# DMA transposes, another spread of the attention units, and a last tile in two halves, in a fused attention and feed-forward kernel

## The chip, the cores and the metric

The kernel runs on one core of one Trainium2 chip. A time is the device time of one execution in microseconds (us). Each run is fast or slow; slow means over 1.5% above the fastest run of the same kernel. Ratios below are taken between fast runs alone; the medians and ranges printed beside them are of all runs, and where slow runs matter they are called that. A profile is of one execution, and its span is a little shorter than the device time: for the kernel before, the profiled execution spans 176.4 us.

## The reference

The input x has 2048 rows of 448 columns. Attention and feed-forward both read the same normalised x, and their results are multiplied.

```python
def _layernorm(x, axis=-1, eps=1e-5):
    m = jnp.mean(x, axis=axis, keepdims=True)
    v = jnp.var(x, axis=axis, keepdims=True)
    return (x - m) / jnp.sqrt(v + eps)
# ... (setup: x is (1, 2048, 448) bf16; wqkv (448, 1344); wo (448, 448); w1 (448, 1792); w2 (1792, 448)) ...
def reference(A_x, A_wqkv, A_wo, B_x, B_w1, B_b1, B_w2, B_b2):
    def _A_ref(x, wqkv, wo):
        B, S, D = x.shape
        H = 16; Dh = D // H
        W, dil = 8, 2
        qkv = (lambda x, *d: x.transpose(*d))((x @ wqkv).reshape(B, S, 3, H, Dh), 2, 0, 3, 1, 4)
        # ... each position attends to 8 positions, two apart, itself and backwards; softmax; times v ...
        return (lambda x, *d: x.transpose(*d))(o, 0, 2, 1, 3).reshape(B, S, D) @ wo
    def _B_ref(x, w1, b1, w2, b2):
        h = jnp.einsum("bsd,df->bsf", x, w1) + b1
        h = _gelu(h)
        return jnp.einsum("bsf,fd->bsd", h, w2) + b2
    x = A_x
    xn = _layernorm(x, axis=-1)
    s = _A_ref(xn, A_wqkv, A_wo)
    g = _silu(_B_ref(xn, B_w1, B_b1, B_w2, B_b2))
    return x + s * g
```

## The kernel before

TensorE (PE) multiplies, ScalarE (ACT) does exponentials, GELU and some copies, VectorE (DVE) the remaining elementwise work, and SyncE (SP) issues the DMAs. The first three, and GpSimd (POOL) with its few constants, follow a hand-written order; SyncE does not, so that the scheduler may move its DMAs. Rows are handled in 16 tiles of 128, in four chunks of four tiles. Even and odd rows are stored apart, so that the dilated attention becomes one over neighbours. It is cut into 17 "units" of 121 queries.

TensorE needs the normalised x with columns on the partitions, so every tile is transposed into `xnT`. For chunk 0 this happens in the prologue. For chunks 1 to 3, the kernel before does it with TensorE, inside the feed-forward block of the chunk before, and VectorE copies the result out of PSUM, the memory that TensorE's products are written to.

All loads but two tiles of x are issued by SyncE, and the trace has them in the order of the program. The sixteen small loads of the output weights `wo` are last among them:

```python
    for dst, c0, c1 in ((wv, 2 * D, 3 * D), (wraw, 0, 2 * D)):
        nc.sync.dma_start(dst[:, 0:3, 0:c1 - c0], A_wqkv[0:384, c0:c1].rearrange("(k p) f -> p k f", p=P))
        nc.sync.dma_start(dst[:64, 3, 0:c1 - c0], A_wqkv[384:448, c0:c1])
    nc.sync.dma_start(b1t[:], B_b1.rearrange("(m f) -> f m", f=P))
    for c0, c1 in ((0, F // 2), (F // 2, F)):
        nc.sync.dma_start(w1[:, 0:3, c0:c1], B_w1[0:384, c0:c1].rearrange("(k p) f -> p k f", p=P))
        for r in (0, 64):
            nc.sync.dma_start(w1[r:r + 64, 3, c0:c1], B_w1[384:448, c0:c1])
        if c0 == 0:
            nc.sync.dma_start(x_sb[1][:, :, :], dram_rows(x_par, 4, 4))
    nc.sync.dma_start(w2[:, :, :], B_w2.rearrange("(m p) c -> p m c", p=P))
    nc.sync.dma_start(b2bc[:], B_b2.rearrange("(o d) -> o d", o=1).to_broadcast((P, D)))
    nc.sync.dma_start(x_sb[2][:, :, :], dram_rows(x_par, 8, 4))
    nc.sync.dma_start(x_sb[3][:, :, :], dram_rows(x_par, 12, 4))
    # ... constants ...
    for g in range(4):
        for h in range(4):
            r = (4 * g + h) * DH
            nc.sync.dma_start(wo[32 * h + 1:32 * h + 1 + DH, g, :], A_wo[r:r + DH, :])
```

The normalisation, the transpose and its copy, and the first reader of the transposed chunk:

```python
    def ln_apply(t):
        nc.vector.tensor_scalar(xnb[t % 4][:, 0:D], xt(t), mv[:, t, 0:1], rstd[:, t:t + 1],
                                op0=ALU.subtract, op1=ALU.mult)

        nc.vector.tensor_copy(xnb[t % 4][:, D:512], xnb[t % 4][:, D - 64:D])

    def ln_tr(t):
        pT = psB.tile([P, KT, P], BF16, name="pT", tag="B")
        for kt in range(KT):
            nc.tensor.transpose(pT[:, kt, :], xnb[t % 4][:, kt * P:(kt + 1) * P], ident[:])
        return pT

    def ln_put(t, pT, copy):
        copy(xnT[:, :, LEAD + t * P:LEAD + (t + 1) * P], pT[:, :, :])
    # ...
    def qk_job(c, g, which, copy):
        ps = psB.tile([P, CH], F32, name="ps_qk", tag="B")
        for kt in range(KT):
            nc.tensor.matmul(ps[:, :], wqk[:, kt, 16 * which + 4 * g:16 * which + 4 * g + 4, :],
                             xnT[:, kt, LEAD + c * CH:LEAD + (c + 1) * CH],
                             start=(kt == 0), stop=(kt == KT - 1))
        copy((qT, kT)[which][:, g, LEAD + c * CH:LEAD + (c + 1) * CH], ps[:, :])
```

One feed-forward block. `gelu` runs on ScalarE, and the products for the next pair of columns can only begin when a PSUM buffer of an earlier pair has been read. `wos` is a list of output tiles that TensorE takes in between:

```python
    def feed_forward_1(c, ps, wos):

        nc.scalar.preload_act_table_set(SET_GELU)
        nx = 4 * (c + 1)
        gelu(0, ps)
        for k in range(0, MT // 2, 2):
            if k:
                ps = ffn1_even(c, k)
                gelu(k, ps)
            if k + 1 < MT // 2:
                ps = ffn1_odd(c, k + 1)
                gelu(k + 1, ps)
            if c + 2 < NC and k < 4:
                ln_stats(nx + 4 + k)
                ln_stats(nx + 5 + k)
            if k in (2, 4):
                if c + 1 < NC:
                    for j in (k - 2, k - 1):
                        ln_put(nx + j, ln_tr(nx + j), nc.vector.tensor_copy)
                if c:
                    silu_job(4 * (c - 1) + k - 2)
                    silu_job(4 * (c - 1) + k - 1)
            for _ in range(2):
                if k >= (2 if c == 3 else 4) and wos:
                    wo_job(wos.pop(0))
        nc.scalar.preload_act_table_set(SET_EXP)
        if c + 2 < NC:
            ln_rstd(nx + 4, 4)
```

An output tile and the second half of an attention unit. `stream_shuffle` copies the softmax sums out of PSUM, ScalarE inverts them with Ln and Exp, and VectorE multiplies:

```python
    def wo_job(t):
        wo_put(t, wo_mm(t))
    # ...
    def qk_unit(b, between=lambda: None):
        # ... 16 score products into two PSUM pairs S, exponentials and masks into E ...
    def av_unit(b, E):
        psO = psB.tile([P, 4, P], F32, name="psO", tag="B")
        for g in range(4):
            for h in range(4):
                nc.tensor.matmul(psO[32 * h:32 * h + 32, g, 0:QW], vw[:, b, 4 * g + h, :],
                                 E[:, h, g, 0:QW], start=True, stop=True)
        n = min(QB, S - QB * b)
        den = work.tile([P, 4, QB], F32, name="den", tag="den", bufs=2)
        nc.vector.stream_shuffle(den[:, :, 0:n], psO[:, :, 0:n], [0] * 32)

        def norm():
            nc.scalar.activation(den[:, :, 0:n], den[:, :, 0:n], ACT.Ln)
            nc.scalar.activation(den[:, :, 0:n], den[:, :, 0:n], ACT.Exp, scale=-1.0)
            nc.vector.tensor_tensor(out=oT[:, :, QB * b:QB * b + n], in0=psO[:, :, 0:n],
                                    in1=den[:, :, 0:n], op=ALU.mult)
        return norm
```

The main loop: a feed-forward block, then the attention units, with the second feed-forward product (`ffn2_job`), the last q and k products and the v products beside them. Three phases take five units each, and two are left for the tail:

```python
        ps = ffn1_even(0, 0)
        for t in range(4, 8):
            ln_apply(t)

        units = iter(range(NB))
        for c in range(3):
            feed_forward_1(c, ps, [[], [0, 1], [2, 3, 4, 5]][c])
            n = c + 1
            beside = [lambda: q_job(n, 3), lambda: k_job(n, 3), lambda: v_job(4 * n), lambda: v_job(4 * n + 1)]
            if c == 2:
                beside[1] = lambda: (k_job(3, 3), v_job(12))
                beside[2] = lambda: v_job(13)
                beside[3] = lambda: v_job(14)
            for g in range(3):
                q_job(n, g)
                k_job(n, g, nc.vector.tensor_copy)
            norm = lambda: None
            for i in range(4):
                b = next(units)
                E = qk_unit(b)
                norm()
                ffn2_job(4 * c + i)
                beside[i]()
                if n + 1 < NC:
                    ln_apply(4 * n + 4 + i)
                norm = av_unit(b, E)
            b = next(units)
            va, vb = 4 * n + 2 + (c == 2), 4 * n + 3 + (c == 2)
            E = qk_unit(b, lambda: v_job(va))
            v_job(vb)
            norm()
            ps = ffn1_even(n, 0)
            norm = av_unit(b, E)
            norm()
        feed_forward_1(3, ps, [6, 7, 8, 9, 10])
        ffn2_job(12)
        E = qk_unit(15)
        g12 = silu_exp_job(12)
        ffn2_job(13)
        g12()
        s11 = wo_mm(11)
        norm = av_unit(15, E)
        wo_put(11, s11)
        E = qk_unit(16)
        g13 = silu_exp_job(13)
        norm()
        y14 = ffn2_job(14, False)
        s12 = wo_mm(12)
        norm = av_unit(16, E)
        g13()
        ffn2_put(14, y14)
        wo_put(12, s12)
        s13 = wo_mm(13)
        norm()
        nc.scalar.preload_act_table_set(SET_GELU)
        wo_put(13, s13)
        silu_job(14)
        y15 = ffn2_job(15, False)
        s14 = wo_mm(14)
        s15 = wo_mm(15)
        ffn2_put(15, y15)
        wo_put(14, s14)
        silu_job(15)
        wo_put(15, s15)
```

The softmax here doesn't subtract the row's maximum and nothing guards it: scores larger than these inputs give would overflow.

## Time and profile before

| kernel before | value |
|---|---|
| device time, median of 3 runs | 177.59 us (177.31 to 180.35, the last a slow run) |
| span of the profile | 176.4 us |
| TensorE busy | 163.9 us, 93% |
| ScalarE, VectorE busy | 71%, 68% |
| start of the q products of chunk 1 | 31.00 us |
| start of the GELU of the last feed-forward block | 143.01 us |
| first scores of the tail, last VectorE instruction | 155.63 us, 173.55 us |

The last three rows are read from the chain of waits and from the timeline of ScalarE.

The page of the profile also cuts the span into 40 slices. Each digit is the busy share of TensorE in tenths, and in the second row the granted clock of TensorE in tenths of full speed. From the kernel before:

```profile
PE   7698999999999989999999989999999999999480
PEclk9999999999999999999999999999999999999998
```

A reader should see that after the first four slices (17.6 us) TensorE is hardly ever free before the tail, and that its recorded clock stays at nine tenths or more until the last slice. This record doesn't show the slow start: the first eight products of 512 columns take 3.48 us, 0.43 us each instead of the 0.22 of later ones, while the view by windows gives a clock of 1.00 from 0.80 to 4.80 us.

### The profile page before, as it was taken

To read this page: it belongs to the slowest core of one execution; us is meant where nothing else is said; L and a number is where in the kernel's file an instruction comes from. 1 tells how busy PE (TensorE), PEld (TensorE's weight loads), DVE (VectorE), ACT (ScalarE), POOL (GpSimd) and SP (SyncE) were. 2 spreads that over 40 slices of the span, in tenths; PEclk is the share of its full clock that TensorE was granted. 3 is DMA by queue.
4 is the path that set the end of the run, shared out by engine and by line. 5 is a ranking of instruction groups with operands and counts; after the bars stand their busy time and mean duration, and the time that the engine had idled before them with its cause. 6 is when DMAs were issued, how large, how long until landed. Compare 5 with 4: busy or idle time off the path is not lost.

```text
span 176.4 us, 3278 instructions
## 1 busy us (share of the span) xinstructions
PE 163.9 (93%) x1324; PEld 75.6 (43%) x1324; DVE 120.0 (68%) x269; ACT 124.7 (71%) x196; POOL 4.5 (3%) x16
## 2 busy tenths in 40 slices
PE   7698999999999989999999989999999999999480
PEld 2343344444454334445454335444555434445140
DVE  6854846667886655977886415987677413978693
ACT  3853397646889699646879699534788699978650
POOL 6030000000000000000000000000000000000000
PEclk9999999999999999999999999999999999999998
DMA  5999972000000000100000000210000000120011
GB/s 145 232 239 320 362 245 50 3 0 4 0 4 0 0 0 4 52 0 4 0 0 6 0 0 0 73 34 0 4 0 0 4 2 0 52 78 30 0 52 52
DMA packets 10991, 9.03 MB, mean 51 GB/s; under 512 B 2593, under 2 KB 10977, under 8 KB 10977
## 3 DMA queue, kind: packets, MB, share of 16 engines
q1 hardware_dynamic: 10688, 8.61, 16.6%
q10 hardware_dynamic: 288, 0.23, 0.4%
q8 instruction: 10, 0.16, 0.4%
q14 instruction: 5, 0.03, 0.1%
HBM read 7.00 MB, written 1.84 MB: 50 GB/s over the span
## 4 chain that ended last, share of the span: by engine, by line
PE 68%; ACT 15%; DVE 7%; SPq 4%; DMA 3%; issue 2%; DVEq 0%
PE ps_y L257 23%; PE ps_h L224 13%; PE ps_qk L188 13%; PE ps_s L288 6%; ACT E L317 4%; PE S L312 3%; PE ps_v L203 3%; DMA x<-in_A_x_dram 3%; PE ps_h L233 3%; ACT hT L239 3%; ACT den L336 2%; PE psO L328 2%; SPq L106 2%; ACT den L335 2%; DVE den L332 2%
## 5 line engine op out<-in xcount | busy, mean ns | idle before, releaser
L317 ACT ACTIVATE E<-S 128x976 bf16<-128x976 f32 x34 | 32.0, 985 | 19.6 <-PE S L312 18.7
L257 PE MATMUL ps_y<-w,hT 128*128 128x448 bf16 x224 | 45.1, 353 | 0.7 <-DVE y L264 0.7
L224 PE MATMUL ps_h<-xnT,w 128*128 128x512 bf16 x168 | 40.3, 380 | 1.5 <-ACT hT L239 1.5
L239 ACT ACTIVATE hT<-ps_h,b1f 128x512 bf16<-128x512 f32 x56 | 33.9, 708 | 2.6 <-PE ps_h L233 2.2
L188 PE MATMUL ps_qk<-xnT,wqk 128*128 128x512 bf16 x128 | 29.4, 379 | 0.6 <-DVE qT L191 0.6
L257 PEld LDWEIGHTS <-hT 128*128 128x128 bf16 x224 | 20.8, 98 | 20.2 <-issue 0.9
L319 DVE TENSOR_TENSOR E<-E,mk_gen 128x976 bf16<-128x976 bf16 x30 | 19.9, 666 | 7.6 <-ACT E L317 7.6
L224 PEld LDWEIGHTS <-w 128*128 128x128 bf16 x168 | 15.4, 98 | 21.4 <-issue 5.7
L337 DVE TENSOR_TENSOR oT<-psO,den 128x484 bf16<-128x484 f32 (+1 forms) x17 | 11.2, 661 | 12.7 <-ACT den L336 12.7
L188 PEld LDWEIGHTS <-wqk 128*128 128x128 bf16 x128 | 12.4, 98 | 15.5 <-issue 1.4
L269 DVE SCALAR_TENSOR_TENSOR g<-th,y 128x448 bf16<-128x448 bf16 x14 | 8.2, 621 | 14.1 <-ACT th L268 14.1
L203 PE MATMUL ps_v<-wv,xnT 128*128 128x448 bf16 x68 | 15.2, 353 | 0.1
L288 PE MATMUL ps_s<-wo,oT 128*128 128x448 bf16 x64 | 13.8, 353 | 1.6 <-DVE oT L337 1.6
L335 ACT ACTIVATE den<-den 128x484 f32<-128x484 f32 (+1 forms) x17 | 10.4, 610 | 5.4 <-DVE den L332 5.4
L191 DVE CAST qT<-ps_qk 128x512 bf16<-128x512 f32 x16 | 10.9, 682 | 3.5 <-PE ps_qk L188 3.5
L156 DVE BATCH_NORM_STATS2 st<-x 128x6 f32<-128x448 bf16 x16 | 9.8, 610 | 5.0 <-DMA x<-in_A_x_dram 5.0
L208 ACT CAST vw<-ps_v 128x448 bf16<-128x448 f32 x17 | 9.1, 536 | 3.9 <-PE ps_v L203 3.8
L332 DVE STREAM_SHUFFLE den<-psO 128x484 f32<-128x484 f32 (+1 forms) x17 | 11.8, 696 | 0.0
L233 PE MATMUL ps_h<-xnT,w 64*128 64x512 bf16 x56 | 10.5, 384 | 0.4
L336 ACT ACTIVATE den<-den 128x484 f32<-128x484 f32 (+1 forms) x17 | 10.3, 605 | 0.5
L264 DVE TENSOR_TENSOR y<-ps_y,b2bc 128x448 f32<-128x448 f32 x16 | 9.9, 618 | 0.9 <-PE ps_y L257 0.8
L294 DVE SCALAR_TENSOR_TENSOR sg<-ps_s,g 128x448 bf16<-128x448 f32 x16 | 9.9, 618 | 0.2
(60 smaller groups left out, 126.5 us busy)
## 6 DMA issues: line engine op xcount, KB each, us to landing
out_dram<-o_t SPq DMA_DIRECT2D x16, 112.0 KB
w<-in_B_w_dram SPq DMA_DIRECT2D x1, 1568.0 KB
w<-in_B_w_dram SPq DMA_DIRECT2D x2, 672.0 KB
x<-in_A_x_dram SPq DMA_DIRECT2D x3, 448.0 KB
wraw<-in_A_wqkv_dram SPq DMA_DIRECT2D x1, 672.0 KB
w<-in_B_w_dram SPq DMA_DIRECT2D x4, 112.0 KB
wo<-in_A_wo_dram SPq DMA_DIRECT2D x16, 24.5 KB
wv<-in_A_wqkv_dram SPq DMA_DIRECT2D x1, 336.0 KB
```

Source lines behind the costliest of these rows:

```text
L188: nc.tensor.matmul(ps[:, :], wqk[:, kt, 16 * which + 4 * g:16 * which + 4 * g + 4, :], xnT[:, kt, LEAD + c * CH:LEAD + (c + 1) * CH], star ...
L203: nc.tensor.matmul(ps[:, :], xnT[:, kt, o:o + P], wv[:, kt, :], start=(kt == 0), stop=(kt == KT - 1))
L224: nc.tensor.matmul(ps[i][:, :], w1[:, kt, m * P:(m + 1) * P], xnT[:, kt, LEAD + c * CH:LEAD + (c + 1) * CH], start=(first and kt == 0), st ...
L233: nc.tensor.matmul(ps[i][:, :], w1[r, 3, m * P:(m + 1) * P], xnT[r, 3, LEAD + c * CH:LEAD + (c + 1) * CH], start=first, stop=not first)
L239: nc.scalar.activation(hT[:, m, :], ps[i][:, :], ACT.Gelu_apprx_tanh, bias=b1f[:, m:m + 1])
L257: nc.tensor.matmul(ps[:, :], hT[:, m, tt * P:(tt + 1) * P], w2[:, m, :], start=(m == 0), stop=(m == MT - 1))
L288: nc.tensor.matmul(ps[:, :], oT[:, g, t * P:(t + 1) * P], wo[:, g, :], start=(g == 0), stop=(g == 3))
L317: nc.scalar.activation(ev, Sp[p2][:, :, :, 0:QW], ACT.Exp, scale=SCALE)
L319: nc.vector.tensor_tensor(out=ev, in0=ev, in1=mkb, op=ALU.mult)
L332: nc.vector.stream_shuffle(den[:, :, 0:n], psO[:, :, 0:n], [0] * 32)
L335: nc.scalar.activation(den[:, :, 0:n], den[:, :, 0:n], ACT.Ln)
L336: nc.scalar.activation(den[:, :, 0:n], den[:, :, 0:n], ACT.Exp, scale=-1.0)
```

## The change

The intent is to free TensorE and VectorE: the 48 transposes of chunks 1 to 3 and the twelve copies behind them become twelve DMA transposes, issued by SyncE as soon as a tile is normalised. The units are placed 5, 5, 6 and 1 instead of 5, 5, 5 and 2, so that the tail has a single one. The output tiles 4 to 7 move out of the feed-forward blocks, to stand beside the units 14 and 15. The last tile is computed in two column halves, each stored by itself, and with the gate multiplied in another order so that less stands behind the tanh. The load of x for chunk 1 is issued earlier.

```diff
 # ...
         nc.sync.dma_start(dst[:64, 3, 0:c1 - c0], A_wqkv[384:448, c0:c1])
+    nc.sync.dma_start(x_sb[1][:, :, :], dram_rows(x_par, 4, 4))
     nc.sync.dma_start(b1t[:], B_b1.rearrange("(m f) -> f m", f=P))
 # ... the same load is removed from behind the first half of w1 ...
 
-    def ln_put(t, pT, copy):
-        copy(xnT[:, :, LEAD + t * P:LEAD + (t + 1) * P], pT[:, :, :])
+    def ln_put(t, pT):
+        nc.scalar.copy(xnT[:, :, LEAD + t * P:LEAD + (t + 1) * P], pT[:, :, :])
+
+    def ln_dma(t):
+        nc.sync.dma_start_transpose(xnT[:, :, LEAD + t * P:LEAD + (t + 1) * P], xnb[t % 4][:, :])
 # ... in the feed-forward block ...
             if k in (2, 4):
-                if c + 1 < NC:
-                    for j in (k - 2, k - 1):
-                        ln_put(nx + j, ln_tr(nx + j), nc.vector.tensor_copy)
                 if c:
                     silu_job(4 * (c - 1) + k - 2)
                     silu_job(4 * (c - 1) + k - 1)
             for _ in range(2):
-                if k >= (2 if c == 3 else 4) and wos:
+                if k >= 4 and wos:
                     wo_job(wos.pop(0))
 # ... busy(8) becomes busy(9), and busy(2) stands behind the first transposes; LEAD 8 becomes 16 ...
         for t in range(4, 8):
             ln_apply(t)
+            ln_dma(t)
 # ...
+        beside = {
+            0: [(ffn2_job, 0, q3, 1), (ffn2_job, 1, k3, 1), (ffn2_job, 2, v_job, 4), (ffn2_job, 3, v_job, 5)],
+            1: [(ffn2_job, 4, q3, 2), (ffn2_job, 5, k3, 2), (ffn2_job, 6, v_job, 8), (ffn2_job, 7, v_job, 9)],
+            2: [(ffn2_job, 8, q3, 3), (ffn2_job, 9, k3, 3, v_job, 12), (ffn2_job, 10, v_job, 13),
+                (ffn2_job, 11, v_job, 14), (wo_job, 4, wo_job, 5, v_job, 15, wo_job, 6)],
+        }
         for c in range(3):
-            feed_forward_1(c, ps, [[], [0, 1], [2, 3, 4, 5]][c])
+            feed_forward_1(c, ps, [[], [0, 1], [2, 3]][c])
             n = c + 1
-            beside = [lambda: q_job(n, 3), lambda: k_job(n, 3), lambda: v_job(4 * n), lambda: v_job(4 * n + 1)]
-            if c == 2:
-                beside[1] = lambda: (k_job(3, 3), v_job(12))
-                beside[2] = lambda: v_job(13)
-                beside[3] = lambda: v_job(14)
             for g in range(3):
                 q_job(n, g)
                 k_job(n, g, nc.vector.tensor_copy)
             norm = lambda: None
-            for i in range(4):
+            for i, jobs in enumerate(beside[c]):
                 b = next(units)
                 E = qk_unit(b)
                 norm()
-                ffn2_job(4 * c + i)
-                beside[i]()
-                if n + 1 < NC:
+                for f, t in zip(jobs[::2], jobs[1::2]):
+                    f(t)
+                if n + 1 < NC and i < 4:
                     ln_apply(4 * n + 4 + i)
+                    ln_dma(4 * n + 4 + i)
                 norm = av_unit(b, E)
             b = next(units)
-            va, vb = 4 * n + 2 + (c == 2), 4 * n + 3 + (c == 2)
-            E = qk_unit(b, lambda: v_job(va))
-            v_job(vb)
-            norm()
+            if c < 2:
+                E = qk_unit(b, lambda: v_job(4 * n + 2))
+                v_job(4 * n + 3)
+                norm()
+            else:
+                E = qk_unit(b, lambda: v_job(16))
+                norm()
+                wo_job(7)
             ps = ffn1_even(n, 0)
             norm = av_unit(b, E)
             norm()
-        feed_forward_1(3, ps, [6, 7, 8, 9, 10])
+        feed_forward_1(3, ps, [8, 9, 10])
         ffn2_job(12)
-        E = qk_unit(15)
+        E = qk_unit(16)
         g12 = silu_exp_job(12)
         ffn2_job(13)
         g12()
         s11 = wo_mm(11)
-        norm = av_unit(15, E)
+        norm = av_unit(16, E)
         wo_put(11, s11)
-        E = qk_unit(16)
-        g13 = silu_exp_job(13)
         norm()
+        nc.scalar.preload_act_table_set(SET_GELU)
         y14 = ffn2_job(14, False)
+        silu_job(13)
         s12 = wo_mm(12)
-        norm = av_unit(16, E)
-        g13()
         ffn2_put(14, y14)
         wo_put(12, s12)
+        silu_job(14)
         s13 = wo_mm(13)
-        norm()
-        nc.scalar.preload_act_table_set(SET_GELU)
         wo_put(13, s13)
-        silu_job(14)
-        y15 = ffn2_job(15, False)
         s14 = wo_mm(14)
+        wo_put(14, s14)
+
+        hw = D // 2
         s15 = wo_mm(15)
-        ffn2_put(15, y15)
-        wo_put(14, s14)
-        silu_job(15)
-        wo_put(15, s15)
+        g = g_sb[15 % NG]
+        th = work.tile([P, D], BF16, name="th", tag="th", bufs=2)
+        o_t = work.tile([P, D], BF16, name="o_t", tag="o_t", bufs=3)
+        for cs in (slice(0, hw), slice(hw, D)):
+            yp = psB.tile([P, hw], F32, name="ps_y15", tag="B")
+            for m in range(MT):
+                nc.tensor.matmul(yp[:, :], hT[:, m, 3 * P:4 * P], w2[:, m, cs],
+                                 start=(m == 0), stop=(m == MT - 1))
+            y = y_sb[:, 3, cs]
+            nc.vector.tensor_tensor(out=y, in0=yp[:, :], in1=b2bc[:, cs], op=ALU.add)
+            nc.scalar.activation(th[:, cs], y, ACT.Tanh, scale=0.5)
+
+            t0 = work.tile([P, hw], F32, name="t0", tag="t0", bufs=2)
+            nc.vector.scalar_tensor_tensor(out=t0[:], in0=s15[:, cs], scalar=0.5, in1=y,
+                                           op0=ALU.mult, op1=ALU.mult)
+            nc.vector.scalar_tensor_tensor(out=g[:, cs], in0=th[:, cs], scalar=1.0, in1=t0[:],
+                                           op0=ALU.add, op1=ALU.mult)
+            nc.vector.tensor_tensor(out=o_t[:, cs], in0=xt(15)[:, cs], in1=g[:, cs], op=ALU.add)
+            nc.sync.dma_start(dram_rows(out_par, 15, 1)[:, 0, cs], o_t[:, cs])
```

## The prediction

> **What bounds the kernel now.** I read the busy shares first, to learn which engine has no room, then the chain that ended last in order of time, to see where that engine is held, then the waits, and last the issue queue of SyncE, because the change puts new work there.
>
> ```profile
> PE 163.9 (93%) x1324; PEld 75.6 (43%) x1324; DVE 120.0 (68%) x269; ACT 124.7 (71%) x196; POOL 4.5 (3%) x16
> ```
>
> TensorE is busy for 163.9 of 176.4 us; the other engines have a third of their time free. So a change helps if it takes work off TensorE where TensorE sets the pace, or closes a gap of TensorE. The listed gaps:
>
> ```profile
> PE ps_s L288 <- DVE oT L337: 1.6, 1, 1.6
> PE ps_h L224 <- ACT hT L239: 1.5, 2, 0.8
> ...
> PE ps_y L257 <- DVE y L264: 0.7, 1, 0.7
> ...
> PE ps_qk L188 <- DVE qT L191: 0.6, 1, 0.6
> ```
>
> Each line is total wait, number of waits, longest one, in us. The first and third lie in the tail (at 164 and 166.5 us), the second is one gap of 0.77 in each of the phases of chunks 1 and 2, and the fourth comes at 16.3 us. Now the chain around the end of the first feed-forward block (start, length, what):
>
> ```profile
> 25.25 0.45 PE pT L172 x8
> ...
> 28.93 0.45 PE pT L172 x8
> 29.38 1.29 PE ps_h L224 x6
> 30.68 0.32 PE ps_h L233 x2
> 31.00 5.29 PE ps_qk L188 x24
> ```
>
> Eight transposes cost TensorE 0.45 us. At 31.00 us it begins the q and k products of chunk 1, which read all 512 transposed columns of that chunk. Next the SyncE queue up to then:
>
> ```profile
> 10.22 0.59 SPq L110 DMA_DIRECT2D x<-in_A_x_dram  x1
> ...
> 18.03 1.77 SPq L114 DMA_DIRECT2D x<-in_A_x_dram  x1
> 19.92 10.17 SPq L134 DMA_DIRECT2D wo<-in_A_wo_dram  x16
> 71.90 102.01 SPq L298 DMA_DIRECT2D out_dram<-o_t  x16
> ```
>
> The sixteen small loads of the output weights occupy the queue from 19.92 to 30.09 us. Whatever follows them in the program can't be issued before. This is the line the whole prediction turns on.
>
> **What the Trainium skill says.** "VectorE: DVE Perf Modes", section "The three transpose paths", gives 390 ns for a 128x128 transpose on TensorE and 1309 ns on the DMA crossbar. The trace of the kernel before has eight in 0.45 us when pipelined, so TensorE is far cheaper here; it has no DMA transpose to compare with. "DMA: Bandwidth & Descriptors", section "Latency and other measured facts", gives 261 GB/s for DMA transposes with a non-contiguous middle dimension: 128 KB in about 0.5 us, so bytes are not the problem. The same page, section "Anatomy of one DMA — SWDGE (gpsimd) path", says that any semaphore wait happens on the issuing sequencer before dispatch: issues of one queue stand in program order. The trace agrees in what it shows: one out-store at a time, each after its data. "TensorE: Matmul & The Clock Gate", section "Part 1: The HAM clock gate (the "warmup" mystery)", says that the clock is half after an idle window of about 3.4 us and full again after about 3.4 us of work. The trace agrees for the start: the first eight 512-column products take 3.48 us, 0.43 each, and later ones come every 0.22. Its later gaps are all under 2 us and show no drop.
>
> **The change part by part.**
>
> *Start.* The load of x for chunk 1 moves ahead of the first half of w1. Its arrival at 15.43 us held VectorE for 2.75 us, VectorE then freed a PSUM buffer late, and TensorE lost 0.64 us at 16.9. I count -0.64. The three extra dummy products lie in TensorE's idle time (it waits for VectorE there): 0.
>
> *Transposes, chunk 1.* 16 TensorE transposes leave, 0.90 us by the chain, all on the path. TensorE would reach the q products at 31.00 - 0.64 - 0.90 = 29.5 us. It then needs four DMA transposes. Their source rows are ready by 23 us, but in the order of the SyncE queue they stand behind the sixteen weight loads, so the first is issued at about 30.1. Moving the x load doesn't move that: the same loads stand in front, and the DMA engines are loaded (share 1.03 to 1.09) until 25 us. For each transpose of four 128x128 blocks I take 1.3 us of queue time, an estimate between a plain issue (0.33 to 0.59 us in the trace) and four times the page's block time; then 1.4 us to land, from the last out-store, which the program's end waits 1.3 us for. That is 30.1 + 4 x 1.3 + 1.4 = 36.7 us. TensorE stands from 29.5 to 36.7 us: 7.2 us idle. Against the 31.00 of before, the q products start 5.7 us later. With a gap of over 3.4 us the clock falls, and the next 3.4 us of work run at half speed: +1.7.
>
> *Transposes, chunks 2 and 3.* Their rows are normalised during the attention units (41 to 54 us and 82 to 94 us on the scale of before) and needed at 70 and 110 us, so the DMA has over 15 us: no wait. Of the two groups of eight in each feed-forward block the first lies just before the 0.77 us gap in which TensorE waits for ScalarE's GELU; without it the gap is only longer (1.2). Only the second counts: 2 x 0.45 = -0.9. The VectorE copies out of PSUM also go (12 x about 0.4 us), on an engine with room: 0.
>
> *Units 5,5,6,1.* Unit 15 and the output products 4 to 7 go before the last feed-forward block. The block of chunk 2 loses eight output matmuls, -1.62. The added stage costs TensorE 0.33 (scores) + 4 x 0.76 (three output tiles, one v) + 0.33 (values) = 3.7. One v copy less (0.43) lies on the ScalarE chain into the block. So the last block's GELU starts 1.62 - 3.7 + 0.43 = 1.65 us later. Inside the last block nothing is won: its k=4 pair must wait for ScalarE to free a PSUM pair, 2.43 us after the GELU start as in the other blocks, against 2.58 with the two output tiles as filler: -0.15.
>
> *Tail.* From the first scores of the tail to the last VectorE instruction the kernel before takes 155.63 to 173.55, 17.9 us, with the 1.6 and 0.7 us gaps. With one unit instead of two I follow the engines: scores at 0, value product at 3.8 to 4.2, shuffle to 5.3, Ln and Exp to 6.5, table load 1.28 to 7.8, tanh 13 to 8.4, then VectorE in order: gate 13 (0.62), bias 14 (0.6), three output tiles at 0.97 each and gate 14 (0.62) to 13.1, and two halves at about 1.45 each (bias, product, gate, add at 224 columns, 0.3 to 0.4 each): 16.0. That is -1.9; TensorE ends before it, so VectorE sets the end.
>
> Sum: q start +5.7 (with -0.64 and -0.90 inside), clock +1.7, chunks 2 and 3 -0.9, units +1.65 - 0.15, tail -1.9: +6.1 us. 177.6 + 6.1 = 183.7 us.
>
> **The rivals.**
>
> *The transposes are in time.* If each costs no more than a plain issue, the last lands at 30.1 + 4 x 0.5 + 1.4 = 33.5: q start +2.5, perhaps a clock drop of 1.7, rest -1.3: 178.9 to 180.5 us. For it: little data, DMA engines idle after 25 us. Against: the order of the queue forbids less. To get a real gain (all savings, no stall: some 174.8 us) the weight loads would have to be out of the queue by about 24 us, and their 10.17 us are measured.
>
> *The transposes are much slower.* If the four blocks of an instruction go one after the other at 1.31 us, a transpose takes 5.2 us and chunk 1 lands at 52: q start +21, about 199 us. Chunks 2 and 3 would still be in time. Nothing in the trace speaks for or against; the page's bandwidth speaks against.
>
> *VectorE becomes the bound in the added stage.* With three output tiles it has 1.34 (masks) + 3 x 0.97 + 0.70 + 0.67 = 5.6 us there against TensorE's 3.7. It has slack before and after, so at most +1 to +2 us, on top of any of these.
>
> *The clock doesn't fall*, because the idle window isn't caught: 182 us.
>
> **Range and chances.** The term that decides is queue time per transpose. 0.5 us gives 179 to 180.5, 1.3 gives 183.7, 2 gives 186.5 and 2.5 gives 188.5. I say 179.3 to 189.5 for 8 in 10. Slower by over 2% means above 181.1, which needs about 0.65 us per transpose with the clock drop and 1.1 without: 0.74. Within 2%: 0.20. Faster by over 2% (below 174.0) needs no stall and a tail better than I count: 0.06.
>
> **What would show it.** In the waits of the new profile: one long wait of TensorE, q product on the DMA of xnT, 5 to 8 us near 30 us. In the SyncE queue: the first transpose after the last output-weight load, at about 30 us, and the spacing of the four. In the first q products after it: about 0.43 us each rather than 0.22. In the blocks of chunks 1 and 2: gaps on the GELU of 1.2 instead of 0.77. At 16 to 17 us: no wait of q on VectorE. In the tail: VectorE busy without break from about the tanh of tile 13. I am wrong if TensorE's wait at 30 us is under 3 us, or if a later phase waits for transposes too.

## The result

| | before | after |
|---|---|---|
| device time, median of 4 runs | 177.93 us (177.31 to 180.35, the last a slow run) | 186.43 us (186.36 to 186.94) |
| ratio of fast runs | 1 | 1.0496, 95% interval 1.0453 to 1.0539 |
| span of the profile | 176.4 us | 185.2 us |
| mean granted clock in the profile | 0.997 | 0.979 |

A ratio here is the mean time of one kernel's fast runs over the mean of the other's in the same rounds, so it is not quite the ratio of the medians. The changed kernel is 5.0% slower, at 186.4 us instead of the predicted 183.7, and inside the predicted range. Its result is correct. The run that was profiled is the slowest of the four (186.94 us, a span of 185.2 us against 184.7 in the others), so that the differences read from the two traces below are some 0.5 us above those of the other runs.

The same parts of the page as above, for the changed kernel. The first line is busy time, share of the span and number of instructions by engine:

```profile
PE 164.3 (89%) x1293; PEld 75.1 (41%) x1293; DVE 116.7 (63%) x261; ACT 123.8 (67%) x195; POOL 4.5 (2%) x16
...
PE   7999993099999997999999979999999877999970
...
PEclk9999999659999999999999999999999999999999
```

The busy time of TensorE has not fallen, although 48 transposes have gone, which at 0.45 us for eight would be 2.7 us. (The count falls by 31 only, since three dummy products and fourteen products of the halved last tile are new.) Some of its other work has become slower. The third line shows a hole in the seventh and eighth slice (28 to 37 us), and the last line a lower clock beside it. That is where the time went. The waits of TensorE name it (total wait, number of waits, longest, in us):

```profile
PE ps_qk L190 <- DMA xnT<-xnb: 7.6, 1, 7.6
PE ps_h L226 <- ACT hT L241: 3.7, 3, 1.2
...
PE ps_s L290 <- ACT vw L210: 1.1, 1, 1.1
PE psO L330 <- DVE oT L339: 1.0, 1, 1.0
```

The first is a single wait of 7.6 us of the q product for a DMA into `xnT`, a transpose. The third and fourth did not exist before, and belong to the stage with units 14 and 15. Now the SyncE queue of the changed kernel (start, time until the last issue of the group ends, what):

```profile
19.94 10.44 SPq L133 DMA_DIRECT2D wo<-in_A_wo_dram  x16
30.49 5.22 SPq L178 DMA_TRANSPOSE xnT<-xnb  x4
```

The first transpose is issued when the sixteenth weight load is out of the queue. From the chain of waits of the changed kernel, in order of time:

```profile
30.49 1.30 SPq L178
...
31.89 1.20 SPq L178
...
33.18 1.22 SPq L178
...
34.49 2.44 DMA xnT<-xnb
36.93 0.14 issue
37.06 7.27 PE ps_qk L190 x24
44.33 0.33 PE S L314 x16
```

Each transpose occupies the queue for 1.2 to 1.3 us, the fourth lands 2.44 us after its issue began, and the q products start at 37.06 us instead of 31.00. Those 24 products then take 7.27 us instead of the 5.29 of before. The table of windows says why (the ninth column, after the five engines, is the clock; the header is that of the view):

```profile
core 0: us, PE busy (x) PEld busy (x) DVE busy (x) ACT busy (x) POOL busy (x), PEclk, DMA share, GB/s
37.00:41.00 4.00, 3.94 (x10) 1.50 (x11) 1.02 (x2) 0.00 (x0) 0.00 (x0) 0.50 0.00 0
41.00:44.30 3.30, 3.30 (x20) 1.32 (x22) 2.44 (x4) 0.00 (x0) 0.00 (x0) 1.00 0.00 0
```

In the first 4 us behind the wait the granted clock is 0.50 and TensorE gets through 10 matmuls; in the next 3.3 us it is 1.00 and it gets through 20.

The milestones of the two traces, in us, with what each stretch adds:

| milestone | before | after | difference | added in this stretch |
|---|---|---|---|---|
| q products of chunk 1 start | 31.00 | 37.06 | +6.06 | +6.06 |
| first scores, unit 0 | 36.28 | 44.33 | +8.05 | +1.99 |
| k=4 pair of chunk 2's block | 103.48 | 111.09 | +7.61 | -0.44 |
| GELU of the last block starts | 143.01 | 154.25 | +11.24 | +3.63 |
| first scores of the tail | 155.63 | 166.76 | +11.13 | -0.11 |
| last VectorE instruction ends | 173.55 | 182.69 | +9.14 | -1.99 |
| span | 176.4 | 185.2 | +8.8 | -0.3 |

The row of the last block's GELU holds two things: eight transposes less in chunk 2's block (-0.45, taken from the block of chunk 1, the row above) and the new placement of units and output tiles, which is therefore +4.1 us. Before the last block's GELU there is one chain: VectorE shuffles the sums of the last unit, ScalarE does Ln, Exp and a table load, and then GELU. The timeline of ScalarE in the kernel before (start, length, what, and in brackets how long it sat idle and for whom):

```profile
140.45 0.61 ACT L335 ACTIVATE den<-den 128x484 f32<-128x484 f32 x1 [1.35 <-DVE den L332]
...
143.01 1.26 ACT L239 ACTIVATE hT<-ps_h,b1f 128x512 bf16<-128x512 f32 x2
```

And in the changed kernel:

```profile
151.70 0.61 ACT L337 ACTIVATE den<-den 128x484 f32<-128x484 f32 x1 [2.31 <-DVE den L334]
...
154.25 1.26 ACT L241 ACTIVATE hT<-ps_h,b1f 128x512 bf16<-128x512 f32 x2
```

From the inversion to the GELU it is 2.56 and 2.55 us; but in the changed kernel ScalarE waits 2.31 us for the shuffle instead of 1.35. The timeline of VectorE in the changed kernel shows what it did ahead of that shuffle:

```profile
143.91 0.66 DVE L339 TENSOR_TENSOR oT<-psO,den 128x484 bf16<-128x484 f32 x1 [0.46 <-ACT den L338]
144.49 0.61 DVE L296 SCALAR_TENSOR_TENSOR sg<-ps_s,g 128x448 bf16<-128x448 f32 x1
145.14 0.39 DVE L299 TENSOR_TENSOR o_t<-x,sg 128x448 bf16<-128x448 bf16 x1
...
149.42 0.67 DVE L339 TENSOR_TENSOR oT<-psO,den 128x484 bf16<-128x484 f32 x1 [0.22 <-ACT den L338]
150.00 0.61 DVE L296 SCALAR_TENSOR_TENSOR sg<-ps_s,g 128x448 bf16<-128x448 f32 x1
150.65 0.39 DVE L299 TENSOR_TENSOR o_t<-x,sg 128x448 bf16<-128x448 bf16 x1
...
150.97 0.70 DVE L334 STREAM_SHUFFLE den<-psO 128x484 f32<-128x484 f32 x1
```

Between 143.91 and 151.67 us VectorE is idle for 0.22 us. Four output tiles of about 1 us each stand in that stretch, the last of them (150.00 to 151.04) directly ahead of the shuffle on which ScalarE waits.

### The profile page after: what moved, and what is told of

The parts are those of the page before. It is cut to its first block, busy times and chain, and to the rows that moved or that the text cites. A ratio compares the mean times of both kernels' runs of the same rounds, so it can differ in the third digit from the quotient of the medians.

```text
span 185.2 us, 3234 instructions
## 1 busy us (share of the span) xinstructions
PE 164.3 (89%) x1293; PEld 75.1 (41%) x1293; DVE 116.7 (63%) x261; ACT 123.8 (67%) x195; POOL 4.5 (2%) x16
## 4 chain that ended last, share of the span: by engine, by line
PE 53%; ACT 20%; SPq 12%; DVE 6%; DMA 6%; issue 2%; DVEq 0%; ACTq 0%
PE ps_y L259 19%; PE ps_qk L190 12%; PE ps_h L226 7%; ACT E L319 5%; DMA x<-in_A_x_dram 5%; ACT hT L241 4%; PE ps_s L290 4%; PE S L314 3%; PE ps_v L205 3%; ACT den L338 3%; SPq L107 3%; ACT den L337 2%; PE psO L330 2%; ACT L353 2%; SPq L111 2%
## 5 line engine op out<-in xcount | busy, mean ns | idle before, releaser
L259 PE MATMUL ps_y<-w,hT 128*128 128x448 bf16 x210 | 42.3, 353 | 0.0
L190 PE MATMUL ps_qk<-xnT,wqk 128*128 128x512 bf16 x128 | 31.2, 397 | 7.6 <-DMA xnT<-xnb 7.6
L259 PEld LDWEIGHTS <-hT 128*128 128x128 bf16 x210 | 19.4, 98 | 18.0
L266 DVE TENSOR_TENSOR y<-ps_y,b2bc 128x448 f32<-128x448 f32 x15 | 9.3, 618 | 0.8 <-PE ps_y L259 0.8
L296 DVE SCALAR_TENSOR_TENSOR sg<-ps_s,g 128x448 bf16<-128x448 f32 x15 | 9.3, 617 | 0.0
```

What stands on the lines that cost most here:

```text
L259: nc.tensor.matmul(ps[:, :], hT[:, m, tt * P:(tt + 1) * P], w2[:, m, :], start=(m == 0), stop=(m == MT - 1))
```

## The experiments

Two theories were to be told apart first. The queue theory: the stall comes from the place of the transposes in the SyncE queue, so it vanishes when the weight loads stand behind them. Its rival: DMA transposes are slow or late in themselves, or wait for their rows. Besides this, the clock, the placement of units and the tail had each been given a size, to be measured apart. Eleven kernels and one repetition ran, all with a correct result. The ratio in each line is to the kernel before in the same rounds. Where two experiments of different rounds are compared, differences of 0.1 to 0.3 us lie inside the intervals of their ratios, and the traces have to decide.

### The stall kept, the clock kept up: e1_warm_stall

```diff
             n = c + 1
+            if c == 0:
+                busy(32)
             for g in range(3):
```

The 32 dummy products fill the wait, so that TensorE is not idle.

> The changed kernel with 32 dummy products of 512 columns put on TensorE in its 7.6 us wait for the transposes of chunk 1. Theory: the first products after the wait take 0.43 us instead of 0.22 because the clock fell in the idle time; the dummies (32 x 0.215 = 6.9 us) keep it up, the wait itself stays (q products start at 37.1 us as before), and the 24 q and k products take 5.3 us instead of 7.3: about 184.4 us, 2.0 less than the changed kernel's 186.4. Rival: the products are slow for another reason (reads of freshly written columns, traffic of the transposes in SBUF): they stay at 7.3 us and the time at 186.4.

It took 185.28 us (185.07 to 185.89), ratio 1.0424 (1.0389 to 1.0458). The chain of waits of this run:

```profile
34.54 2.43 DMA xnT<-xnb
...
37.11 5.34 PE ps_qk L190 x24
```

The transpose lands as before, but the 24 products take 5.34 us instead of 7.27. So the loss behind the stall is the clock, and the idle wait caused it. In time, 1.2 us were won rather than the 1.9 of the traces. The profiled run of the changed kernel was 0.5 us slower than its others, and the repetition below makes the rest plausible: the slow stretch differs between profiles, and costs 1.5 us there.

### The weight loads behind the transposes: e2_wo_late

```diff
-    for g in range(4):
-        for h in range(4):
-            r = (4 * g + h) * DH
-            nc.sync.dma_start(wo[32 * h + 1:32 * h + 1 + DH, g, :], A_wo[r:r + DH, :])
 # ...
             ln_apply(t)
             ln_dma(t)
+        for g in range(4):
+            for h in range(4):
+                r = (4 * g + h) * DH
+                nc.sync.dma_start(wo[32 * h + 1:32 * h + 1 + DH, g, :], A_wo[r:r + DH, :])
```

> The changed kernel with one thing moved: the loads of the output weights stand behind the first four transposes in the program (two of the sixteen stay ahead). Theory (order of the SyncE queue): the transposes are issued by about 21 to 26 us, land by 29.4, and TensorE does not wait: q products start at 29.4 us, without the clock drop: 186.4 - 7.6 - 2.0 = 176.8 us. Rival (the transposes themselves are slow, or queue behind the loads of w2 and x in the DMA engines until long after 25 us): a wait of several us stays, 180 us or more.

It took 177.22 us (177.18 to 177.24), ratio 0.9964 (0.9940 to 0.9989). Its SyncE queue:

```profile
19.59 2.75 SPq L425 DMA_DIRECT2D wo<-in_A_wo_dram  x2
22.45 5.22 SPq L174 DMA_TRANSPOSE xnT<-xnb  x4
27.72 6.12 SPq L425 DMA_DIRECT2D wo<-in_A_wo_dram  x14
```

And its chain of waits:

```profile
28.98 0.32 PE ps_h L231 x2
29.30 4.64 PE ps_qk L186 x21
```

The four transposes take the same 5.22 us of queue, but from 22.45 us on, and TensorE goes from the feed-forward products into the q products without a wait. The same work in another order is worth 9.2 us. That decides for the queue theory. (Two of the sixteen loads were still put ahead, though they stand behind the transposes in the program: SyncE's order is the scheduler's.) The rest of the change, without any stall, is then no gain to speak of: 0.4%.

### The transposes back on TensorE: e3_pe_transposes

```diff
-    def ln_dma(t):
-        nc.sync.dma_start_transpose(xnT[:, :, LEAD + t * P:LEAD + (t + 1) * P], xnb[t % 4][:, :])
 # ...
             if k in (2, 4):
+                if c + 1 < NC:
+                    for j in (k - 2, k - 1):
+                        ln_put(nx + j, ln_tr(nx + j), nc.vector.tensor_copy)
 # ... and the calls of ln_dma removed ...
```

> The changed kernel with the transposes of chunks 1 to 3 back on TensorE and all else kept. Theory: q products start at 31.0 - 0.68 = 30.3 us (6.75 earlier), no clock drop (-2.0), 0.45 more in each of the blocks of chunks 1 and 2 (+0.9): 186.4 - 7.85 = 178.5 us. So the rest of the change (unit placement and tail) is slower than the kernel before by 0.9 us in spite of the 0.68 won at the start. Rival (the rest of the change is a gain of 2 us as its tail suggests): 175.5 us.

It took 179.13 us (179.10 to 179.20), ratio 1.0072 (1.0041 to 1.0102). The difference between this kernel and the one ahead of it, from the same rounds, is what DMA transposes are worth when they are in time: 1.9 us, where the prediction had 0.90 and 0.9. And it shows the rest of the change by itself, units, tail and the early x load: 1.1 us slower than the kernel before (1.3 by the ratio), where 0.9 had been expected; the rival, a gain of 2 us, is out. A tail that is 2 us shorter in the trace does not show in the sum, so something in it costs more than predicted.

### The old placement and tail, with the early transposes: e4_wo_late_old_units

```diff
 # e2_wo_late, and in it
-            feed_forward_1(c, ps, [[], [0, 1], [2, 3]][c])
+            feed_forward_1(c, ps, [[], [0, 1], [2, 3, 4, 5]][c])
 # ... five units per phase, two in the tail, the last tile whole: all of it as in the kernel before ...
```

> As e2, and with the unit placement and the tail of the kernel before. Theory: from the GELU-bound pair of chunk 2's block to the end the kernel before takes 72.9 us, the changed one 74.1 although it saves one group of transposes (0.45), so placement and tail together cost 1.65 us: 176.8 - 1.65 = 175.2 us, the best so far. Rival (the added stage was only slow because of the DMA transposes or the shifted time): equal to e2 or up to 2 us slower than it.

It took 176.21 us in the median, ratio 0.9907 (0.9855 to 0.9960), but on two levels: 175.46 and 175.56, and 176.86 and 176.91. The GELU of its last block starts at 140.8 us, where e2_wo_late has 144.5. So the new placement costs 3.7 us up to there, close to the 4.1 of the milestones, and the prediction's 1.65 is too small. The spans of the profiles (173.8 and 175.5 us) differ by 1.7 us, which is this cost less what the tail gives back. The expected gain of 1.65 us over e2_wo_late is met by the faster of the two levels only.

### Output tiles away from the last units: e5_wo_late_spread

If VectorE's output tiles are what delays the shuffle, moving them to units where VectorE has room must help.

```diff
 # e2_wo_late, and in it
-            2: [(ffn2_job, 8, q3, 3), (ffn2_job, 9, k3, 3, v_job, 12), (ffn2_job, 10, v_job, 13),
-                (ffn2_job, 11, v_job, 14), (wo_job, 4, wo_job, 5, v_job, 15, wo_job, 6)],
+            2: [(wo_job, 4, wo_job, 5, q3, 3, k3, 3, v_job, 12), (ffn2_job, 8, wo_job, 6), (ffn2_job, 9, v_job, 13),
+                (ffn2_job, 10, v_job, 14), (ffn2_job, 11, v_job, 15)],
```

> As e2, with the output tiles 4 to 6 spread over the units of phase 2 (two in the first, one in the second) so that a feed-forward tile stays beside unit 14. Theory: in the changed kernel VectorE has 5.6 us of work in the added stage against 3.7 on TensorE, and TensorE waits 1.1 + 1.0 us there and ScalarE 2.3 us for the shuffle; spread out, no stage has more on VectorE than on TensorE, and the GELU of the last block starts some 2 us earlier: 177.2 - 2.0 = 175.2 us, level with e4. Rival (the added stage is long because of ScalarE's own chain of exponentials and denominators, which is the same in both): under 0.7 us gained.

It took 176.01 us (175.98 to 176.16), ratio 0.9897 (0.9870 to 0.9924), 1.2 us less than e2_wo_late. That lies between the 2.0 expected and the rival's 0.7. The GELU starts at 143.4 instead of 144.5 us. Tile 7 is still ahead of the last shuffle here, and ScalarE's wait for it is still 2.31 us: the gain lies in the stage of unit 14, where TensorE's wait of 1.1 us for ScalarE's v copy is gone and the scores of the last unit start at 134.67 instead of 135.81 us.

### The same work in the same stage, in another order: e6_wo_late_norm_after

The rival for that loss was order: not that VectorE has too much to do, but that the output tiles stand at a bad place behind the norm.

```diff
 # e2_wo_late, and in it
-                (ffn2_job, 11, v_job, 14), (wo_job, 4, wo_job, 5, v_job, 15, wo_job, 6)],
+                (ffn2_job, 11, v_job, 14), (v_job, 15)],
 # ...
                 E = qk_unit(b)
+                if i == 4:
+                    for t in (4, 5, 6):
+                        wo_job(t)
                 norm()
```

> As e2, with the three output tiles of the added stage issued ahead of the normalisation of unit 13 instead of behind it; same work in the same stage. If the sum of VectorE's work in the stage sets its length, only VectorE's wait of 0.46 us for the denominator is filled: 176.7 us. If the order does it (the output tiles held behind the denominator of unit 13, and the v copy behind it on ScalarE), 1 to 2 us: 175.2 to 176.2.

It took 177.02 us (176.93 to 177.09), ratio 0.9951 (0.9924 to 0.9978): 0.2 us less than e2_wo_late, the GELU at 144.3 instead of 144.5 us, and a new wait of 0.8 us of a v product for VectorE, in place of the 1.1 us for ScalarE. So this other order wins next to nothing, which speaks for the amount of work in the stage; further orders weren't tried.

### The halves of the last tile, in the old tail: e7_old_units_halves

```diff
 # e4_wo_late_old_units, and in its tail
-        y15 = ffn2_job(15, False)
         s14 = wo_mm(14)
+        wo_put(14, s14)
+        # ... the last tile in two halves, as in the changed kernel ...
```

> As e4, with the last tile in two column halves and the gate multiplied in the other order, its output products ahead of the second feed-forward product as in the change: the tail part of the change alone. Theory: after the end of TensorE 1.55 us of VectorE and ScalarE work on 224 columns instead of 2.05, and the last store is half as large (the changed kernel's end came 2.5 us after its last VectorE instruction instead of 2.85): 0.8 us less than e4, 174.7 to 175.4. Rival: the last output tiles fill VectorE up to the end of TensorE, and the halves, which double the number of instructions, win nothing: as e4.

It took 176.54 us (176.23 to 176.86), ratio 0.9924 (0.9892 to 0.9956), and so nothing less than e4_wo_late_old_units. This was a miss. The waits of TensorE in this kernel show where it went:

```profile
PE ps_s L286 <- DVE oT L335: 2.2, 2, 1.6
```

In the kernel before there is one such wait, of 1.6 us. Here there is a second, of 0.58 us: with the halves, output tile 15 is multiplied ahead of the last feed-forward products, and it needs the rows that the last of the two units, unit 16, has just normalised. The halves had been written for a tail with one unit.

### Only the early load of x: e8_before_x_early

```diff
 # the kernel before, and in it
+    nc.sync.dma_start(x_sb[1][:, :, :], dram_rows(x_par, 4, 4))
     nc.sync.dma_start(b1t[:], B_b1.rearrange("(m f) -> f m", f=P))
 # ...
-        if c0 == 0:
-            nc.sync.dma_start(x_sb[1][:, :, :], dram_rows(x_par, 4, 4))
```

> The kernel before, with only the load of x for chunk 1 moved ahead of w1. Theory: TensorE's wait of 0.64 us at 16.9 us goes and nothing else changes: 0.68 us faster than the kernel before, about 177.3. Rival: w1 comes late and TensorE waits for it instead: 0 or slower.

It took 178.29 us (177.17 to 180.17), ratio 0.9993 (0.9940 to 1.0045), which is inconclusive as a time. In the trace the step does what was predicted: the wait of q for VectorE is gone, and the GELU of the last block starts at 142.19 instead of 143.01 us. The profiled run lost this again in its tail. Its last feed-forward tile, in the timeline of TensorE:

```profile
166.40 4.19 PE L256 MATMUL ps_y<-w,hT 128*128 128x448 bf16 x14 [0.69 <-DVE y L263]
```

The same tile in the kernel before:

```profile
167.21 2.81 PE L257 MATMUL ps_y<-w,hT 128*128 128x448 bf16 x14 [0.69 <-DVE y L264]
```

The same fourteen matmuls behind the same gap take 4.19 us and 2.81 us. The windows of the run of e8_before_x_early say that it was the clock (0.50, the first figure after POOL's). By the windows beside these it fell at about 165.8 us and came back at about 169.2:

```profile
167.00:168.00 1.00, 1.00 (x4) 0.44 (x3) 1.00 (x3) 0.99 (x2) 0.00 (x0) 0.50 0.00 0
168.00:169.00 1.00, 1.00 (x5) 0.33 (x3) 0.97 (x3) 0.42 (x1) 0.00 (x0) 0.50 0.34 115
```

No gap near it is longer than 1.62 us. Gaps of this length occur in the tail of each kernel with two units there (before, e4, e7, e8). These kernels are also the ones that scatter: over 1.4 us for e4 with clocks of 0.989 in its longer runs and 0.997 and over in its shorter ones, and up to 180.4 us in slow runs of the kernel before, which have a clock of 0.988. That a dip in the tail is the cause in those runs too is likely but not shown, since only one profile caught it; and e8_before_x_early has a run of 178.62 us at a full clock.

### No output tile beside the last two units: e9_spread_all

```diff
 # e5_wo_late_spread, and in it
-                (ffn2_job, 10, v_job, 14), (ffn2_job, 11, v_job, 15)],
+                (ffn2_job, 10, v_job, 14, wo_job, 7), (ffn2_job, 11, v_job, 15)],
 # ...
                 E = qk_unit(b, lambda: v_job(16))
                 norm()
-                wo_job(7)
```

> As e5, with output tile 7 taken out of the last stage of phase 2 too and put beside unit 13. Theory: in e5 that tile holds a PSUM buffer (TensorE waits 1.0 us for the value product of unit 15) and stands ahead of unit 15's shuffle on VectorE; without it the shuffle comes 1.5 us earlier and so does the last block's GELU, for 0.76 us of TensorE work moved ahead: 0.75 us less than e5, 175.3 us, and no wait of psO on VectorE. Rival (ScalarE's chain sets the GELU start): as e5, 176.0.

It took 175.91 us (175.75 to 175.96), ratio 0.9877 (0.9852 to 0.9902), only 0.1 us less than e5_wo_late_spread. The last inversion on ScalarE:

```profile
140.65 0.61 ACT L333 ACTIVATE den<-den 128x484 f32<-128x484 f32 x1 [1.35 <-DVE den L330]
```

ScalarE again waits 1.35 us for the shuffle, as in the kernel before: no output tile stands in front of it. In e5_wo_late_spread it was:

```profile
140.84 0.61 ACT L333 ACTIVATE den<-den 128x484 f32<-128x484 f32 x1 [2.31 <-DVE den L330]
```

Yet the GELU starts only 0.2 us earlier, at 143.21 instead of 143.40 us. The rival had named this outcome, with ScalarE's chain as the reason, but the trace gives another: tile 7, 0.76 us of TensorE, now stands ahead of the last unit's scores, which start at 135.44 instead of 134.67 us. From there to the GELU it is 7.77 instead of 8.73 us, so that 0.96 us is won and 0.77 paid for it. The GELU comes 2.4 us later than in e4_wo_late_old_units. The scores of the last unit there and here:

```profile
132.59 0.40 PE L310 MATMUL S<-qT,kT 28*128 28x122 bf16 x16
```

```profile
135.44 0.40 PE L310 MATMUL S<-qT,kT 28*128 28x122 bf16 x16
```

These 2.85 us are TensorE's own work: one unit more (0.66), four output tiles and a v product (5 x 0.76), less the two output tiles in the block of chunk 2 (1.62), which makes 2.84. From the scores to the GELU it is 0.43 us less, the v copy that is missing there. In time the two kernels can't be told apart (0.9877 and 0.9907, with intervals that overlap): the new placement costs before the last block what the shorter tail gives back.

### Output tiles as filler for the gap that the transposes left: e10_spread_all_fill

Without transposes on TensorE, and with output tiles taken only from k=4 on, the k=4 pair waits 1.25 us for GELU in each of the blocks of chunks 1 to 3. In the kernel before it was 0.77 us in the first two, and nothing in the last. The output tiles of a block can stand in that gap if they are taken from k=2 on.

```diff
 # e9_spread_all, and in it
-                if k >= 4 and wos:
+                if k >= 2 and wos:
```

> As e9, with the two output tiles of each feed-forward block issued before the pair of products that waits for the GELU instead of after the next two pairs, as the kernel before does in its last block only. Theory: without the TensorE transposes the wait there has grown from 0.77 to 1.24 us in each of three blocks, 3.7 in all; two output tiles (1.5 us) fill it: -1.2 in each of the blocks of chunks 1 and 2, little in the last, where ScalarE sets the end: about 2.5 us less than e9, 172.8 us. Rival (ScalarE sets the length of all three blocks, or the VectorE gates come too late and hold PSUM): under 0.8 us.

It took 173.93 us (173.89 to 174.00), ratio 0.9768 (0.9741 to 0.9795), and is the best kernel. The gap in the block of chunk 1, in the timeline of TensorE in e9_spread_all:

```profile
62.11 1.46 PE L222 MATMUL ps_h<-xnT,w 128*128 128x512 bf16 x5 [1.25 <-ACT hT L237]
```

The same stretch in e10_spread_all_fill:

```profile
60.57 1.68 PE L286 MATMUL ps_s<-wo,oT 128*128 128x448 bf16 x8
62.08 1.46 PE L222 MATMUL ps_h<-xnT,w 128*128 128x512 bf16 x5
...
66.38 1.46 PE L222 MATMUL ps_h<-xnT,w 128*128 128x512 bf16 x6 [0.90 <-ACT hT L237]
```

The two output tiles take the place of the first gap. Where they stood before, behind the next six products, a gap of 0.90 us comes up instead. So the blocks of chunks 1 and 2 win about 0.4 us each, and that of chunk 3, which has a third tile to put into the later gap, wins 1.1 of its 1.25. Over the kernel the waits for GELU fall from 3.7 us in three to 1.8 us in two, which is the gain of 2.0 us. Expected were 2.5, most of it in the blocks of chunks 1 and 2 and little in the last; it came the other way round. The same filler with the old placement (e4_wo_late_old_units has two of these gaps) was not run, so that the best kernel doesn't show the new placement to be the better one.

### The changed kernel once more: e11_after_again

The kernel is unchanged here, so there is no diff.

> The changed kernel once more, on the chip of e9 and e10 and with a new profile. If the moment at which the clock comes back after the 7.6 us wait depends on where the wait falls[...], the number of 0.43 us products after it may differ from the first profile (span 185.2), as the other runs' span of 184.7 suggests; if not, the same 24 products in 7.3 us. The time 186.4 either way within 0.5.

It took 187.30 us (186.95 to 188.06), ratio 1.0521 (1.0475 to 1.0566). From its waits:

```profile
PE ps_qk L190 <- DMA xnT<-xnb: 8.7, 1, 8.7
```

The transposes were issued 1 us later than in the first profile (31.44 us), the q products started at 38.12 us, and seven products ran slowly instead of nine, so that the 24 took 6.82 us instead of 7.27. The stall is the same in kind, and its length varies by about 1 us from one profile to the next. The time was expected at 186.4 us within 0.5, and missed that by 0.4.

### The best kernel with a whole last tile: e12_fill_whole_tile

```diff
 # e10_spread_all_fill, and in its tail
-        hw = D // 2
         s15 = wo_mm(15)
-        # ... two halves ...
+        y15 = ffn2_job(15, False)
+        ffn2_put(15, y15)
+        silu_job(15)
+        wo_put(15, s15)
```

> As e10 (173.9 us), with the last tile in one piece and the gate multiplied in the old order, all else kept: what the column halves bring when there is one unit in the tail. Theory: VectorE is busy without a break up to the end of TensorE, so the first half's work of the halved form starts no earlier than the whole tile's, and the two forms end level within 0.1 us (0.62 + 0.58 + 0.62 + 0.65 + 0.39 after TensorE's end against eight half-sized steps from 0.1 us before it); the half-sized last store saves the 0.34 us seen between before and after: 174.2 us. Rival (the halves overlap with TensorE as intended): 0.8 to 1.2 us, 174.7 to 175.1.

It took 174.27 us (174.16 to 174.44), ratio 0.9784 (0.9756 to 0.9812). So the halves bring about 0.3 us when the tail has a single unit, which the ratios of two different rounds don't separate from noise, but the traces support. The last VectorE instruction ends at 170.06 us here and at 169.72 with halves, and from it to the end of the span it is 2.54 and 2.58 us. Of these 0.34 us, 0.12 were there at the GELU of the last block already, so that the tail itself is about 0.2 us shorter. This gain lies in VectorE's work overlapping with the last products and not, as the expectation had it, in the last store being smaller.

## Why the prediction was right and where it was off

**The stall of TensorE was right in place, cause and size.** The transposes were put behind the weight loads at 30.1 us (measured 30.49), at 1.3 us of queue each (1.20 to 1.30), with the last landing at 36.7 us (36.93) and TensorE idle for 7.2 us (7.6). The q products start 6.06 us later against 5.7 predicted. e2_wo_late shows the cause: the same transposes ahead of the loads give no wait. The rivals "in time" and "much slower" fall by the same measurements. A weak point remains in how this was found: 1.3 us was an estimate between two figures, not a measurement, and the range was wide because of it. That it fell on the measured value is in part luck.

**The clock was right.** +1.7 us predicted, +1.99 in the profile of the result and +1.5 (6.82 less 5.29) in the repetition; e1_warm_stall shows that idleness causes it. By the windows of the result's trace the clock fell at about 34.2 us, 4.8 us after TensorE went idle, and came back at about 41.0, 3.9 us into the work, where the prediction had taken 3.4 us for both. The rival "the clock doesn't fall" is out.

**The early x load and the transposes were right.** The loss at 16.9 us is gone; in e8_before_x_early the last block is 0.8 us earlier by it alone. The block of chunk 1 gives 0.44 us of the 0.45 predicted (that of chunk 2 wasn't measured by itself), and all transposes together 1.9 us against 1.8, by e2 and e3 of the same rounds. That the gap on GELU would grow from 0.77 to 1.2 us in the blocks of chunks 1 and 2 was right as well.

**The term for the units was mis-sized.** The step "the last block's GELU starts 1.62 - 3.7 + 0.43 = 1.65 us later" (with its signs turned round: 3.7 - 1.62 - 0.43 is meant) failed: it is 4.1 us by the milestones and 3.7 by e4 against e2. The step counted TensorE's work in the added stage and took that as its length. VectorE had 5.6 us of work in it by the prediction's own count, which it gave to a rival with the note that slack before and after would leave at most 1 to 2 us. The trace shows no slack after: from 143.91 to 151.67 us VectorE is idle for 0.22 us. The start of the last unit's scores divides the 2.4 us by which the step was short, before and after:

```profile
134.89 0.34 PE S L312 x14
```

```profile
145.60 0.34 PE S L314 x14
```

From the k=4 pair of chunk 2's block to these scores 31.41 us became 34.51, which is 3.55 us more once the 0.45 of transposes is put back, where the step's TensorE work gives 3.7 - 1.62 = 2.08. So 1.5 us was lost in the stage of unit 14; 1.12 of it is TensorE's wait for a v copy that ScalarE makes only after its inversion. From the scores to the GELU 8.12 us became 8.65, where the step had 0.43 less: 0.96 us was lost to output tile 7, which VectorE finishes ahead of the last shuffle. The experiments confirm both. Spreading the output tiles over earlier units (e5) wins 1.1 us, all of it before those scores, while reordering them within the stage (e6) wins 0.2. Taking tile 7 away (e9) wins 0.96 us behind the scores and costs its 0.76 us of TensorE ahead of them. In e9, where VectorE keeps up, the GELU is 2.4 us later than in e4, and the step's 1.65 with this 0.76 makes 2.4: TensorE's count was right, and what failed was to take it for the length of stages that other engines end.

**The tail was right.** -1.9 us predicted, -1.99 measured. VectorE sets its end, as predicted. Of this, the halves are 0.2 to 0.3 us, by the traces of e10 and e12. With the end of the program, 0.3 us more was won than predicted.

**The sum.** Predicted +6.1 us, measured +8.8 in the spans: the start is 0.4 us off, the clock 0.3, the units 2.4, and tail and end -0.4. These deviations add up to the difference within 0.1 us. By the medians of all runs it is +8.5. The range of 179.3 to 189.5 us held, because it was drawn wide for the queue time of a transpose, which was in fact well met; the error came from another term that had no width of its own.

## What to carry to other kernels

Here the transposes arrived as late as everything issued ahead of them in SyncE's queue (the first at 30.49 us, behind sixteen loads): before moving work to a DMA, read in the profile when the queue is free, and put loads that are needed later behind it (worth 9.2 us here). When work is taken off the busiest engine, look for the engine whose result ends the stage, and count that engine's work in it rather than that of the busiest. And a gap that the removed work used to fill is worth nothing until other work is moved into it: here that was 2.0 of the 3.3 us from e2_wo_late to the best kernel.

## What the Trainium skill lacked or had wrong

- "VectorE: DVE Perf Modes", section "The three transpose paths", gives one time for a 128x128 block on each path (390 ns on TensorE, 1309 ns by DMA), and doesn't say how it scales or which part of it holds the issuing queue; no page gives the issue time of a DMA transpose of this size on trn2 (the trn3 part of "DMA: Bandwidth & Descriptors" has sequencer cycles of "previous generations", for other transfers). Here one of four blocks held the queue for 1.20 to 1.30 us and landed 2.44 us after its issue began, while eight transposes on TensorE took 0.45 us together. At 128 KB every 1.2 to 1.3 us that is about 100 GB/s, well under the 261 GB/s that the prediction quotes, from which its 0.5 us per transpose is an estimate. The four took the same 5.22 us of queue in e2_wo_late, at another time and with other loads still under way, which points to the issue and not the bytes as what set the pace.
- "TensorE: Matmul & The Clock Gate", section "HAM oscillation — how this bites in real kernels", puts the rule as no idle gaps of TensorE over about 3.4 us. In the profile of e8_before_x_early the clock was 0.50 from about 165.8 to 169.2 us by the windows, with no longer gaps near it than 1.62 and 0.69 us, and fell within the second of them. The section after it, "A second HAM failure mode: psum-queue depth-cycling", tells of such drops through short gaps between groups of matmuls, which fits in kind, but gives no length from which on they count. That the slow stretch varies (nine and seven products after the same kind of wait) agrees with "Part 1: The HAM clock gate (the "warmup" mystery)" on the same page, which has 6, 11 or 14 slow products at the start of one kernel in different runs.
- None of the pages drawn on here sizes the scatter of a whole kernel's time on an undisturbed core: the kernels with one unit in the tail and no stall stayed within 0.3 us in their rounds, the kernel before within 1.8 us in its fast runs (177.17 to 178.90), with slow runs 2 us above.
